# A top-k attention and expert-layer kernel: another latency in its planner, another wait for the first transposes, and SyncE's last reads in another order

## The chip, the cores and the metric

The kernel runs on one core of one Trainium2 chip. The metric is the device time of one launch in microseconds. Before the change its median is 869.37 us over three runs (869.3 to 869.62). The profiled execution spans 867.1 us. The core has five engines that run side by side: TensorE (PE, matmuls and transposes), VectorE (DVE), ScalarE (ACT), GpSimd (POOL) and SyncE (SP, which issues DMAs here).

## The reference

Attention in which each query keeps its 32 best keys, and behind it an expert layer with a squared ReLU:

```python
# q, k, v: (8 batches, 8 heads, 576 positions, 64)
scores = scale * np.matmul(q, k.transpose(0, 1, 3, 2))
kth = np.partition(scores, -top_k, axis=-1)[..., -top_k:-top_k + 1]   # top_k = 32
mask = scores >= kth
scores = np.where(mask, scores, -1000000000.0)
attn = softmax(scores)                      # written out with max, exp and sum
x = np.matmul(attn, v)                      # then (8*576 tokens, 8*64 = 512)
h = x @ w_in                                # 512 -> 2048
g = np.maximum(h, 0.0) ** 2
out = g @ w_out                             # 2048 -> 512
```

## The kernel before

The kernel works in 144 blocks. A block is 128 queries of two heads: PE computes two rows of 576 scores per query into `ps_s`, ACT copies them to `s`, and DVE finds the 32nd largest of each row. It takes the eight largest of a part (`Max`), strikes them out (`MatchReplace`), three times over parts of growing width (104, 124, 272 columns), and then takes the eight largest of all 576 (`kth`). Parts and folds are made with maxima and with integer adds and subtracts on DVE, ACT and GpSimd (`m`, `t1`, `t2`, `f`).

ACT then makes a mask `w` for each of the two heads, PE transposes scores and adds the masks, ACT takes the exponential (`p`), PE multiplies with v (`vb,p`), and the expert layer follows for a chunk of tokens when all four pairs of heads have reached it (`xt,win`, then `wo,g`).

None of this is written in the order in which it runs. Every operation is recorded with an engine, an assumed duration and a priority, and a list scheduler written in Python orders each engine's operations ahead of the launch; semaphores are put in from that order. On the chip each engine runs its list strictly in order. This is the part of the scheduler in which the assumed latency stands:

```python
def schedule(self, t0=0.0, latency=0.12, own=0.07):
    # ... (cut)
                    for v in x.users:
                        left[v] -= 1
                        lat = 0 if x not in v.deps else (own if x.eng != "pe" else .25) if v.eng == x.eng else latency
                        readyat[v] = max(readyat[v], t + lat)
```

Masks and transposes of a block (L720 and L449/L452 in the profile):

```python
                for i in range(2):
                    pl.op("act", .77, tw + .8 * i, lambda i=i: act.activation(
                        at(wt)[:, i, :], at(st)[:, i, :], ACTF.Relu, bias=kth[:, i, n:n + 1], scale=-1.0),
                        r=[st], w=[wt], take=[wt] if i == 0 else [], after=[ks[i]])
    # ... (cut)
            o_t = pl.op("pe", .68, tt, lambda: flip([0, 128, 256, 384], 0), r=[st, wt], w=[e], take=[e, pt])
            o_t = pl.op("pe", .68, tt + .1, lambda: flip([640, 768, 896, 1024], 4), r=[st, wt], w=[e], order=[o_t])
            pl.op("pe", .2, tt + .2, lambda: flip([512], 8), r=[st, wt], w=[e, e9], take=[e9], order=[o_t])
```

The expert layer of a chunk: `xt,win` matmuls, ReLU on ACT, and the square on DVE, GpSimd or ACT. The last chunks have 128 tokens each: 64 matmuls of 128 columns (`xt,win`), four squares, 16 matmuls of 512 columns (`wo,g`), one copy and one store.

```python
                pl.op("act", .19 + w_ / 1200, tf + lag + .5, fr, r=[hh], w=[g])
                if end:                                  # the very last chunk
                    pl.op("dve", ...)                    # g * g
                elif last or i * SQ % 8 < SQ:            # other chunks of the last batch, and some
                    pl.op("gp", ...)                     # g * g
                else:
                    pl.op("act", ...)                    # Square
```

While PE has nothing to do at the start, it plays 87 warm-up matmuls of 512 columns (`ps<-ident_bf`), which write two spare PSUM banks that are also used for transposes of q and k.

At the end a verdict is formed: were 32 keys found in each row in this fast way, and are the sums in range? If not, a fallback program that does it all in a slower way (the `again` plan) is run. Every engine reads the verdict from memory and branches:

```python
        def emit(e, eng):
            em.via(main, e)
            em.emit(main, e, eng)
            if e == "sp":
                for kk, vv in stored(main).items():
                    eng.wait_ge(em.sem(kk), vv)          # all stores of the output
            eng.wait_ge(em.sems["dve"], flagged.idx[1])
            val = eng.value_load(flag[0:1, 0:1], min_val=0, max_val=P)
            with eng.If(val > 0):
                em.emit(again, e, eng)
                # ... (cut)
```

Of the kernel before, what the change touches and what calls it, by code (L numbers as in the profile page):

```python
# [291 lines left out]
def bass_top_k_attn__then__act_relu_squared_kernel(  # L292
# [24 lines left out]
            return nc.alloc_sbuf_tensor(name, shape, dt)  # L317
        return [nc.alloc_sbuf_tensor(f"{name}{i}", shape, dt) for i in range(n)]

    PER = 5.55  # L320
    T0 = 12.0
    LEAD = 39.88
    ME = 21.85
    MQ = 19.61
    MP = 18.0
    MA = 18.27
    SQ = 5.15
    TA = 7.2
    TW = -0.14
    TL = 18.33  # L330
    WARM = 8
    WP = 6.49
    BW = 1
    WSTEP = 1.2
    WEND = 70
    NL = 31.89
    WD = 3.33
    WC = 1.75
    WA = 1.13
    WN = 6  # L340
    NBO = 3.81
    LAG = 12.93
    STEP = 2.98
    LATE = 2.07
    LAGL = 17.86

    ident32 = sb("ident32", [P, P])
    ident_bf = sb("ident_bf", [P, P], BF16)
# [10 lines left out]
    fone = sb("fone", [P, 4])  # L359
# [31 lines left out]
    def tile(nm):  # L391
        return Tile(pools[nm])
# [4 lines left out]
    def bank(t, i=0):  # L397
        return ps32[:, BASE[t.pool.name] + t.slot + i, :]
# [8 lines left out]
    em = Emitter(nc)  # L407
# [48 lines left out]
    def build(full, weights, pl):  # L456
# [129 lines left out]
        def top_k(gi, qks, tg):  # L586
# [53 lines left out]
            ks = []  # L640
# [72 lines left out]
                        eighth(kth, i), at(f)[:, i, :]), hold=[f]))  # L713
            kths.extend(ks)
            tw = tg + PER - TW
            wt = tile("w")
            if not full:

                for i in range(2):
                    pl.op("act", .77, tw + .8 * i, lambda i=i: act.activation(  # L720
                        at(wt)[:, i, :], at(st)[:, i, :], ACTF.Relu, bias=kth[:, i, n:n + 1], scale=-1.0),
                        r=[st], w=[wt], take=[wt] if i == 0 else [], after=[ks[i]])
                return st, wt

            for i in range(2):
                o = pl.op("gp", .75, tw + 1.3 * i, lambda i=i: gp.tensor_scalar(
# [2 lines left out]
                pl.op("gp", .75, tw + 1.3 * i + .65, lambda i=i: gp.tensor_scalar(  # L729
                    at(wt)[:, i, :], at(f)[:, i, :], BIG, at(sh)[:, i:i + 1], ALU.min, ALU.max),  # L730
                    r=[sh], hold=[f], after=[o], w=[wt], take=[wt] if i == 0 else [])
            return st, wt

        minus = neg_bf if full else steep_bf

        def attend(gi, st, wt, tt):

            e, e9, pt = Tile(ps_e), Tile(ps_q), tile("p")

            def flip(cols, i0):  # L740
                sf, wf = (at(t)[:, :, :].rearrange("p i c -> p (i c)") for t in (st, wt))
                outs = [(banks(e)[:, 128 * (i0 + i):128 * (i0 + i) + 128], c, (i0 + i) % 4 == 0)
                        for i, c in enumerate(cols)]
                for o, c, start in outs:
                    tr(o, sf[:, c:c + 128], ident32[:, :], start=start, stop=True)
                for o, c, start in outs:
                    ins = mm(o, wf[:, c:c + 128], minus[:, :], False)
                return ins


            o_t = pl.op("pe", .68, tt, lambda: flip([0, 128, 256, 384], 0), r=[st, wt], w=[e], take=[e, pt])
            o_t = pl.op("pe", .68, tt + .1, lambda: flip([640, 768, 896, 1024], 4), r=[st, wt], w=[e], order=[o_t])
            pl.op("pe", .2, tt + .2, lambda: flip([512], 8), r=[st, wt], w=[e, e9], take=[e9], order=[o_t])
            pl.op("act", 1.15, tt + 1, lambda: act.activation(  # L754
                at(pt)[:, :, :].rearrange("p k q -> p (k q)"), banks(e)[:, 0:2 * S], ACTF.Exp, scale=0.125),
                r=[e, e9], w=[pt])
            return pt
# [57 lines left out]
        def feed(chunk, xt, tm, step):  # L815

            nt = sum(n_ for _, _, n_ in chunk)
            b = chunk[-1][0]
            last, end = b == NB - 1, chunk is CHUNKS[-1]
            kf = max(1, 512 // nt)  # L820
            lag = 0 if end else LAGL if last else LAG
            gs = [tile("g") for _ in range(NFB // kf)]
            for i, g in enumerate(gs):
                hh = Tile(psum)

                def fh(hh=hh, i=i):
                    for f in range(kf):
                        fb = kf * i + f
                        for ct in range(NCT):
                            ins = mm(bank(hh)[:, nt * f:nt * f + nt], win[:, ct, 128 * fb:128 * fb + 128],  # L830
                                     at(xt)[:, ct, 0:nt], ct == 0 and f == 0)
                    return ins

                def fr(hh=hh, g=g):
                    return act.activation(at(g)[:, 0:kf * nt], bank(hh)[:, 0:kf * nt], ACTF.Relu)  # L835

                tf = tm + step * i
                w_ = kf * nt
                ho = pl.op("pe", .03 + kf * 4 * (nt / 2340 + .002), tf + lag, fh, r=[xt], w=[hh], take=[hh, g],
                           after=weights if chunk not in FIRST else weights and weights[NCT * (kf * i // 8):][:NCT],  # L840
                           nbf=tf if not last else 0)
                if chunk in FIRST and weights:
                    first_h.append(ho)
                pl.op("act", .19 + w_ / 1200, tf + lag + .5, fr, r=[hh], w=[g])
                if end:
                    pl.op("dve", .1 + w_ / 1900, tf + lag + .8, lambda g=g: vec.tensor_tensor(
                        at(g)[:, 0:w_], at(g)[:, 0:w_], at(g)[:, 0:w_], ALU.mult), u=[g])
# [45 lines left out]
        for b in range(NB):  # L893
            seq, stages = batch_order(b)
            pairs, held = {}, {}
            last = b == NB - 1
            for hp, gi in seq:
                tg = T0 + PER * state["n"]
                hps = (hp, hp if gi != Z else hp + 1)
                for x in hps:  # L900
                    if x not in pairs:
                        pairs[x] = load_pair(b, x, tg)
                st, wt = top_k(gi, [pairs[x][0] for x in hps], tg)
                if state.get("more"):
                    state.pop("more")()
                tt = tg + PER + 2 - TA - TL * max(0, 1 - (NGRP - state["n"]) / NL)
                pt = attend(gi, st, wt, tt)
                js = [gi] if gi == Z else [g for g in stages if gi in g][0]
                held.setdefault((hp, js[0]), []).append((pt, [pairs[x][1] for x in hps]))
                if gi != js[-1]:  # L910
                    continue
                r0, n_ = 128 * js[0], 128 * len(js) if gi != Z else 64
                i, col = place(b, r0, n_)
                first = xts[i] is None
                if first:
                    xts[i] = tile("xz" if len(CHUNKS[i]) > 1 else "xt")
                collect(gi, held[hp, js[0]], (xts[i], col, first), hp, tt)
                left[i] -= n_ * (2 if gi == Z else 1)
                if left[i] == 0:
# [53 lines left out]
    def verdict(pl, kths, rzs):  # L973
# [11 lines left out]
            fone[:, 1:2], fone[:, 1:2], 1e30, None, ALU.is_gt), after=[e])  # L985
        f = pl.op("dve", .1, 1e6, lambda: vec.tensor_scalar(
            fone[:, 2:3], fone[:, 2:3], 1e-30, None, ALU.is_lt), after=[f])
        g = pl.op("pe", .1, 1e6, lambda: pe.matmul(bank(t)[0:1, 0:3], fone[:, 3:4], fone[:, 0:3],
                                                   start=True, stop=True), w=[t], take=[t], after=[d, e, f])
        return pl.op("dve", .1, 1e6, lambda: vec.tensor_reduce(flag[:, :], bank(t)[0:1, 0:3], AX.X, ALU.max), r=[t])  # L990

# [6 lines left out]
    for o in main.ops[n_pre:]:  # L998
        if o.eng == "sp" and o.takes and o.takes[0].pool.name == "rv":
            o.deps.update(zeros)  # L1000
        if o.eng == "pe":
            o.deps.update(early if n < 7 else early + pre)
            n += 1
    span = main.schedule()
    assert all(o.takes[1].slot < NG - 4 * NWS for o in first_h)
    em.number(main)
    again = Plan()
# [7 lines left out]
    with nc.Block() as blk:  # L1015
        def emit(e, eng):
            em.via(main, e)
            em.emit(main, e, eng)
            if e == "sp":
                for kk, vv in stored(main).items():  # L1020
                    eng.wait_ge(em.sem(kk), vv)
            eng.wait_ge(em.sems["dve"], flagged.idx[1])
            val = eng.value_load(flag[0:1, 0:1], min_val=0, max_val=P)
            with eng.If(val > 0):
                em.emit(again, e, eng)
                if e == "sp":
                    for kk, vv in stored(again).items():
                        eng.wait_ge(em.sem(kk), vv)

        @blk.gpsimd  # L1030
        def _(g_):
            emit("gp", g_)

        @blk.tensor
        def _(pe_):
            emit("pe", pe_)
# [40 lines left out]
```

## Time and profile before

| engine | busy us | share of the 867.1 us | instructions |
|---|---|---|---|
| PE | 823.6 | 95% | 7998 |
| DVE | 824.2 | 95% | 3414 |
| POOL | 788.2 | 91% | 826 |
| ACT | 760.2 | 88% | 1261 |

The DMA engines move 48.21 MB at a mean of 56 GB/s. By the page's chain of work that ended last, DVE holds 66% of the span, PE 21%, ACT 8%, and 5% is "issue".

How to read the lines below: in a timeline a line has start, length, engine, source line, operation, output and inputs with shape, and in brackets the idle time of the engine before it and who ended it. "PE ps L449" is any matmul, "L452" any transpose, for two helper functions issue them all; what they are is told by the tiles behind the arrow. In a row of windows there are the stretch, its length, and busy time with the number of instructions for PE, PEld (the load of weights), DVE, ACT and POOL, then the granted clock, the DMA share and GB/s. A name with a q at the end (SPq, PEldq) is an engine's sequencer.

### The profile page before, as it was taken

What the parts mean: (1) busy time and instruction counts of PE and PEld (TensorE: products, weight loads), DVE (VectorE), ACT (ScalarE), POOL (GpSimd) and SP (SyncE); (2) the same over time, 40 slices, a digit from 0 to 9 for tenths busy, and PEclk for the clock granted to TensorE, in tenths of its full rate; (3) what the DMA queues carried; (4) which work ended last, traced back from release to release, by engine and by line L of the source; (5) the groups of instructions that cost most, each with busy time, mean ns of one, the idle gap of its engine ahead of it and who ended that gap; (6) DMA issues with size and microseconds to landing.
All of it is one profiled execution on the core that took longest, in us unless ns stands there. A gap on an engine that the chain in (4) does not pass through costs nothing.

```text
span 867.1 us, 22631 instructions
## 1 busy us (share of the span) xinstructions
PE 823.6 (95%) x7998; PEld 609.9 (70%) x8057; DVE 824.2 (95%) x3414; ACT 760.2 (88%) x1261; POOL 788.2 (91%) x826
## 2 busy tenths in 40 slices
PE   8898899999999999999999999999999999999996
PEld 3565677667776777767778677776778767687774
DVE  3899999999999999999999999999999999999970
ACT  3788999889998899989999799998989889898873
POOL 6798999999999989999999989999999988998961
PEclk9999999999999999999999999999999999999999
DMA  7583422011310223012130121301231021000001
GB/s 180 120 198 101 126 49 62 27 41 35 91 43 14 60 64 76 21 34 62 33 79 16 39 68 43 97 14 41 57 82 30 14 51 32 26 2 14 26 14 41
DMA packets 126985, 48.21 MB, mean 56 GB/s; under 512 B 119184, under 2 KB 119184, under 8 KB 126864
## 3 DMA queue, kind: packets, MB, share of 16 engines
q1 hardware_dynamic: 126192, 46.52, 21.4%
q8 instruction: 65, 1.06, 0.5%
q14 instruction: 56, 0.46, 0.2%
q10 hardware_dynamic: 672, 0.16, 0.1%
HBM read 37.22 MB, written 9.44 MB: 54 GB/s over the span
## 4 chain that ended last, share of the span: by engine, by line
DVE 66%; PE 21%; ACT 8%; issue 5%; POOL 1%; DVEq 0%; POOLq 0%
DVE f L709 21%; DVE c L705 17%; PE ps L449 15%; DVE kth L712 13%; PE ps L452 5%; DVE ps L678 5%; DVE f L688 5%; DVE m L678 5%; ACT p L754 2%; ACT w L720 1%; ACT s L622 1%; ACT g L835 1%; DVE rzall L783 1%; ACT qk L579 0%; ACT g L852 0%
## 5 line engine op out<-in xcount | busy, mean ns | idle before, releaser
L709 DVE MATCH_REPLACE8 f<-c,f 128x104 f32<-128x104 f32 (+2 forms) x864 | 268.1, 317 | 0.0
L705 DVE MAX8 c<-f 128x8 f32<-128x104 f32 (+2 forms) x864 | 244.7, 321 | 0.1
L720 ACT ACTIVATE w<-s,kth 128x576 bf16<-128x576 f32 x288 | 223.4, 786 | 22.5 <-DVE kth L712 21.6
L452 PE MATMUL ps<-ident,s 128*128 128x128 f32 x1296 | 222.0, 280 | 9.2 <-ACT p L754 5.7
L673 POOL TENSOR_TENSOR t<-s 128x576 int32<-128x576 int32 x144 | 202.5, 1411 | 19.7 <-ACT s L622 19.6
L449 PE MATMUL ps<-qk 64*128 64x64 f32 (+3 forms) x1280 | 207.0, 442 | 2.9 <-DVE m L678 2.5
L712 DVE MAX8 kth<-f 128x8 f32<-128x576 f32 x288 | 208.5, 750 | 0.0
L673 POOL TENSOR_TENSOR f<-t,m 128x576 int32<-128x576 int32 x144 | 203.0, 1410 | 0.0
L449 PEld LDWEIGHTS ps<-qk 64*128 64x128 f32 (+1 forms) x1280 | 128.1, 175 | 77.4 <-issue 60.4
L622 ACT COPY s<-ps 128x1152 f32<-128x1152 f32 x144 | 161.4, 1121 | 22.7 <-PE ps L449 22.4
L754 ACT ACTIVATE p<-ps 128x1152 bf16<-128x1152 f32 x144 | 163.4, 1135 | 13.5 <-PE ps L449 12.6
L452 PEld LDWEIGHTS ps<-ident,s 128*128 128x128 f32 x1296 | 143.1, 141 | 34.2 <-ACT p L754 11.0
L449 PE MATMUL ps<-steep_bf,w 128*128 128x128 bf16 x1296 | 139.9, 219 | 0.0
L673 POOL TENSOR_TENSOR t<-m 128x288 int32<-128x288 int32 x144 | 114.8, 797 | 18.8 <-ACT m L686 14.4
L449 PE MATMUL ps<-wo,g 128*128 128x512 bf16 x517 | 127.6, 379 | 4.1 <-issue 1.0
L449 PE MATMUL ps<-xt,win 128*128 128x256 bf16 (+1 forms) x1152 | 127.0, 261 | 4.1 <-ACT xt L809 2.3
L673 POOL TENSOR_TENSOR f<-t,f 128x288 int32<-128x288 int32 x144 | 114.7, 797 | 0.1
L449 PEld LDWEIGHTS ps<-xt,win 128*128 128x128 bf16 x1152 | 97.4, 98 | 19.6 <-ACT xt L809 3.7
L449 PEld LDWEIGHTS ps<-steep_bf,w 128*128 128x128 bf16 x1296 | 105.1, 100 | 4.0
L849 POOL TENSOR_TENSOR g<-g 128x512 bf16<-128x512 bf16 x92 | 95.3, 1040 | 7.6 <-ACT g L835 7.3
L835 ACT ACTIVATE g<-ps 128x512 bf16<-128x512 f32 x144 | 85.8, 607 | 5.6 <-PE ps L449 4.4
L449 PEld LDWEIGHTS ps<-wo,g 128*128 128x128 bf16 x576 | 51.8, 98 | 48.5 <-ACT g L835 0.5
(67 smaller groups left out, 913.5 us busy)
## 6 DMA issues: line engine op xcount, KB each, us to landing
rv<-in_v_dram SPq DMA_DIRECT2D x64, 128.0 KB, 2.5
out_dram<-o SPq DMA_DIRECT2D x32, 256.0 KB, 2.1
rk<-in_k_dram SPq DMA_DIRECT2D x63, 128.0 KB, 2.5
rq<-in_q_dram SPq DMA_DIRECT2D x62, 128.0 KB, 2.6
g<-in_moe_w_in_dram SPq DMA_DIRECT2D x8, 512.0 KB, 4.3
g<-in_moe_w_out_dram SPq DMA_DIRECT2D x8, 512.0 KB, 3.9
rv<-in_v_dram SPq DMA_DIRECT2D x96, 16.0 KB, 2.2
rq<-in_q_dram SPq DMA_DIRECT2D x32, 32.0 KB, 2.6
```

The costliest lines, as they stand in the source:

```text
L449: return pe.matmul(o, l, r, start=start, stop=stop, skip_group_check=True)
L452: return pe.matmul(o, i, ident, is_transpose=True, skip_group_check=True, **kw)
L622: cp = [pl.op("act", 1.2, tg - LEAD + 1, lambda: act.copy(at(st)[:, :, :], two(banks(ss), SECOND, S)), r=[ss], w=[st])]
L673: return pl.op("gp", dur, prio, lambda: gp.tensor_tensor(o().bitcast(I32), x().bitcast(I32), y().bitcast(I32), op), **kw)
L678: return vec.tensor_tensor(o, two(banks(ss)[:, a:], SECOND + HALF, QUART), two(at(st)[:, 0, HALF + a:], HALF, QUART), ALU.max)
L705: lambda i=i, t=t, c0=c0, c1=c1: vec.max(eighth(t, i), at(f)[:, i, c0:c1]),
L709: lambda i=i, t=t, c0=c0, c1=c1: vec.match_replace(at(f)[:, i, c0:c1], eighth(t, i), at(f)[:, i, c0:c1], NEG), hold=[f])]
L712: ks.append(chain(kth, i, prev[i] + [low], .665, lambda i=i: vec.max(eighth(kth, i), at(f)[:, i, :]), hold=[f]))
L720: pl.op("act", .77, tw + .8 * i, lambda i=i: act.activation(at(wt)[:, i, :], at(st)[:, i, :], ACTF.Relu, bias=kth[:, i, n:n + 1], scale=-1.0),
L754: pl.op("act", 1.15, tt + 1, lambda: act.activation(at(pt)[:, :, :].rearrange("p k q -> p (k q)"), banks(e)[:, 0:2 * S], ACTF.Exp, scale=0 ...
L835: return act.activation(at(g)[:, 0:kf * nt], bank(hh)[:, 0:kf * nt], ACTF.Relu)
L849: pl.op("gp", .15 + w_ / 480, tf + lag + 1, lambda g=g: gp.tensor_tensor(at(g)[:, 0:w_], at(g)[:, 0:w_], at(g)[:, 0:w_], ALU.mult), u=[g])
```

## The change

1. The planner assumes 0.25 us between an operation and one on another engine that needs it, instead of 0.12 us. The order of all five engines is planned anew with it, and the offsets of the priorities (when scores, folds, weights and expert work are wanted) are set anew to go with it.
2. The first four transposes of a block (128-column pieces 0 to 3, all of the first head) wait for the first of the two masks, not for both.
3. SyncE reads the verdict first and waits for the stores afterwards, so that the reading and the branch lie beside the last store. The verdict's matmul no longer has the lowest priority on PE.
4. The squares of the last chunk but one are done by DVE as well.

The diff, with cuts:

```diff
-    PER = 5.55
+    PER = 5.54
-    LEAD = 39.88
-    ME = 21.85
-    MQ = 19.61
+    LEAD = 38.17
+    ME = 19.82
+    MQ = 18.93
-    MA = 18.27
-    SQ = 5.15
+    MA = 21.24
+    SQ = 5.71
-    TW = -0.14
-    TL = 18.33
+    TW = 0.23
+    TL = 15.79
-    WP = 6.49
+    WP = 5.93
-    NL = 31.89
-    WD = 3.33
-    WC = 1.75
+    NL = 36.79
+    WD = 1.68
+    WC = 2.44
-    LATE = 2.07
-    LAGL = 17.86
+    LATE = 2.51
+    LAGL = 21.59
 ...
-            wt = tile("w")
+            wt, masks = tile("w"), []
-                    pl.op("act", .77, tw + .8 * i, lambda i=i: act.activation(
+                    masks[i:] = [pl.op("act", .77, tw + .8 * i, lambda i=i: act.activation(
 ...
-            o_t = pl.op("pe", .68, tt, lambda: flip([0, 128, 256, 384], 0), r=[st, wt], w=[e], take=[e, pt])
+            own = dict(r=[st], hold=[wt], after=ws_[:1]) if ws_ else dict(r=[st, wt])
+            o_t = pl.op("pe", .68, tt, lambda: flip([0, 128, 256, 384], 0), w=[e], take=[e, pt], **own)
 ...
+            direct = chunk in CHUNKS[-2:]
-                if end:
+                if direct:
                     pl.op("dve", .1 + w_ / 1900, ...
 ...
-        g = pl.op("pe", .1, 1e6, lambda: pe.matmul(bank(t)[0:1, 0:3], fone[:, 3:4], fone[:, 0:3],
+        g = pl.op("pe", .1, 0, lambda: pe.matmul(bank(t)[0:1, 0:3], fone[:, 3:4], fone[:, 0:3],
 ...
-    span = main.schedule()
+    span = main.schedule(latency=.25)
 ...
-            if e == "sp":
-                for kk, vv in stored(main).items():
-                    eng.wait_ge(em.sem(kk), vv)
             eng.wait_ge(em.sems["dve"], flagged.idx[1])
             val = eng.value_load(flag[0:1, 0:1], min_val=0, max_val=P)
             with eng.If(val > 0):
+                if e == "sp":
+                    for kk, vv in stored(main).items():
+                        eng.wait_ge(em.sem(kk), vv)
                 em.emit(again, e, eng)
                 # ... (cut)
+            if e == "sp":
+                for kk, vv in stored(main).items():
+                    eng.wait_ge(em.sem(kk), vv)
```

More of the change, by code (lines that the diff above doesn't have):

```diff
@@ L715, in top_k @@
             tw = tg + PER - TW
-            wt = tile("w")
+            wt, masks = tile("w"), []
             if not full:
                 for i in range(2):
-                    pl.op("act", .77, tw + .8 * i, lambda i=i: act.activation(
+                    masks[i:] = [pl.op("act", .77, tw + .8 * i, lambda i=i: act.activation(
                         at(wt)[:, i, :], at(st)[:, i, :], ACTF.Relu, bias=kth[:, i, n:n + 1], scale=-1.0),
-                        r=[st], w=[wt], take=[wt] if i == 0 else [], after=[ks[i]])
-                return st, wt
+                        r=[st], w=[wt], take=[wt] if i == 0 else [], after=[ks[i]])]
+                return st, wt, masks
             for i in range(2):
@@ L731, in top_k, with attend @@
                     r=[sh], hold=[f], after=[o], w=[wt], take=[wt] if i == 0 else [])
-            return st, wt
+            return st, wt, masks
         minus = neg_bf if full else steep_bf
-        def attend(gi, st, wt, tt):
+        def attend(gi, st, wt, tt, ws_):
             e, e9, pt = Tile(ps_e), Tile(ps_q), tile("p")
@@ L902, in build @@
                         pairs[x] = load_pair(b, x, tg)
-                st, wt = top_k(gi, [pairs[x][0] for x in hps], tg)
+                st, wt, ws_ = top_k(gi, [pairs[x][0] for x in hps], tg)
                 if state.get("more"):
@@ L906, in build @@
                 tt = tg + PER + 2 - TA - TL * max(0, 1 - (NGRP - state["n"]) / NL)
-                pt = attend(gi, st, wt, tt)
+                pt = attend(gi, st, wt, tt, ws_)
                 js = [gi] if gi == Z else [g for g in stages if gi in g][0]
```

## The prediction

> **What bounds the kernel now.** I read the page's busy times and slices first, then a table of windows, then the idle times of VectorE (DVE) in order of time, then the last instructions of TensorE (PE), ScalarE (ACT) and SyncE. From the page:
>
> ```profile
> span 867.1 us, 22631 instructions
> PE 823.6 (95%) x7998; PEld 609.9 (70%) x8057; DVE 824.2 (95%) x3414; ACT 760.2 (88%) x1261; POOL 788.2 (91%) x826
> DVE  3899999999999999999999999999999999999970
> ```
>
> DVE is full except in the first two slices and in the last two. The windows say how full (busy us, instructions; in the order PE, PEld, DVE, ACT, POOL):
>
> ```profile
> 0.00:10.00 10.00, 7.24 (x29) 3.09 (x29) 0.69 (x1) 2.49 (x5) 4.28 (x30) 1.00 0.59 137
> 10.00:20.00 10.00, 9.52 (x43) 3.96 (x42) 6.30 (x25) 4.29 (x7) 8.63 (x9) 1.00 0.88 208
> 20.00:30.00 10.00, 9.11 (x56) 5.06 (x54) 7.46 (x29) 8.01 (x13) 5.79 (x7) 1.00 0.47 107
> ...
> 500.00:600.00 100.00, 96.34 (x958) 73.50 (x966) 99.85 (x412) 92.53 (x155) 93.83 (x96) 1.00 0.22 54
> ...
> 850.00:867.00 17.00, 10.36 (x94) 6.24 (x92) 2.00 (x5) 4.01 (x7) 1.66 (x2) 0.95 0.10 36
> ```
>
> From about 30 to 836 us DVE sets the pace: 144 blocks with no idle worth the name. Its whole idle time is 867.1 - 824.2 = 42.9 us: 9.3 + 3.7 + 2.5 in the first 30 us, about 2.5 scattered, and some 25 after the last threshold. So the change can win at the start, at the end, and hardly between. The start, from DVE's timeline (start, length, what, idle before it and who ended it):
>
> ```profile
> 10.44 0.47 DVE L678 TENSOR_TENSOR ps<-ps,s 128x288 f32<-128x288 f32 x1 [2.93 <-ACT s L622]
> 15.42 0.47 DVE L678 TENSOR_TENSOR ps<-ps,s 128x288 f32<-128x288 f32 x1 [3.12 <-ACT s L622]
> ...
> 26.07 0.47 DVE L678 TENSOR_TENSOR ps<-ps,s 128x288 f32<-128x288 f32 x1 [1.40 <-ACT p L754]
> ...
> 29.49 0.47 DVE L678 TENSOR_TENSOR ps<-ps,s 128x288 f32<-128x288 f32 x1 [1.11 <-ACT s L622]
> ```
>
> Blocks 1 to 4 each wait for their scores, which wait for PE, which plays warm-up matmuls in between. The end, from the timeline of all engines; K, the end of the last threshold, is 834.85 + 1.42 = 836.27:
>
> ```profile
> 834.85 1.42 DVE L712 MAX8 kth<-f 128x8 f32<-128x576 f32 x2
> ...
> 847.85 5.53 PE L449 MATMUL ps<-xt,win 128*128 128x128 bf16 x96 [0.63 <-ACT g L835]
> ...
> 853.43 6.86 PE L449 MATMUL ps<-wo,g 128*128 128x512 bf16 x31
> ...
> 860.33 0.59 ACT L869 COPY o<-ps 128x512 f32<-128x512 f32 x1 [2.00 <-PE ps L449]
> ```
>
> After K it is PE that bounds: 24 us of expert-layer matmuls with under 1.5 us of gaps. Then SyncE, from its lines in the source view (ns min/median/max, when):
>
> ```profile
> L1022 SPq EVENT_SEMAPHORE  x1: 1962/1962/1962, 861.3 to 861.3; - x1
> L1023 SPq TENSOR_LOAD <-flag x1: 465/465/465, 863.3 to 863.3; - x1
> L1024 SPq COMPARE_BRANCH  x1: 45/45/45, 864.2 to 864.2; - x1
> L1024 PEldq COMPARE_BRANCH  x1: 4025/4025/4025, 861.5 to 861.5; - x1
> L1015 PEldq DRAIN  x1: 73/73/73, 865.6 to 865.6; - x1
> L1015 SPq DRAIN  x1: 53/53/53, 866.9 to 866.9; - x1
> ```
>
> The last store is issued at 860.94; SyncE waits 1.96 us for it, only then loads the verdict, branches at 864.2, and drains at 866.9. Everybody else has been done since 865.6.
>
> [...]2.7 us from SyncE's branch to its drain, with transfers in the instruction queues, although the branch itself takes 0.045 us. [...]
>
> **The change part by part.**
>
> *SyncE reads the verdict first.* Removed from the end: load, register operations, branch and fetch standing behind the store's 1.96 us. Now SyncE loads at 861.27 (issue 860.94 + 0.33), branches 0.9 us later (863.3 to 864.2 before) at 862.15 and is ready 2.7 us later, at 864.85; the store landed at 863.3. But PE drained at 865.6, 5.0 us after it read the flag at 860.6. The verdict's matmul now stands among the tail's matmuls instead of behind them, so PE reads the flag when its last matmul is issued, some 0.5 us earlier: about 865.1. PE, not SyncE, then ends the kernel, at about 865.1 + 0.2. Worth 867.1 - 865.3 = -1.8 us.
>
> *The start, walked through the changed instruction order with durations of this trace.* The transposes of the rest of the first queries now stand before the first scores: one more warm-up, then 0.69 us to the scores, which start at about 8.7 (7.89 before). Copy to s: 10.1 to 11.2; DVE starts block 1 at 11.25 (10.44): +0.8. Between first and second scores there are now 11 warm-ups instead of 8, but they alternate between two PSUM banks (each waits for the last but one); such a run went at 0.22 us each in the trace (13 from 14.14 on), while the 8, which mostly wait for the one just before, took 3.09 us. Second scores: 10.0 + 11 x 0.22 + 0.2 = 12.65 (12.87). DVE gets block 2 at 15.2 (15.42). It then stalls about 0.3 us, because ACT now converts a weight tile (1.05 us) before the copy into m that DVE needs; block 1 is done at 20.85 (20.80). Block 3's scores need the second pair's keys: I get 20.85 for their start (21.87), s ready at 23.4, a stall of 0.7 in place of 1.40. Block 4's s is ready when DVE gets there, about 28.7: about 0.1 in place of 1.11. Block 3 then ends at 33.8 against 34.88 before. The start is worth -1.1 us; the two later stalls (0.92 at 42.0 and 0.86 at 65.5) may go or stay, -0.3.
>
> *Twice the latency, new offsets.* No instruction is added: the same 87 warm-ups, the same matmuls, the same 144 blocks on DVE. Only their order and waits differ. For the last 30 blocks I added up, at each block's transposes, how much expert work (0.061 us per 128-column matmul, 0.215 per 512-column one, from 6.87 us for 32) is still to come. In the changed order PE is level with before around blocks 100 to 120, 1 to 6 us ahead from 124 to 136, and 2.6 us ahead at the last block. From its first transposes on, PE has: before, 48 x 0.215 + 7.5 for 128 + 3.1 of attention = 20.9 (trace: 839.49 to 860.30); now, 36 x 0.215 + 7.5 + 2.9 = 18.2. But 12 of the 512-column matmuls have moved to just before, and there the stretch grows from 4.3 (835.20 to 839.49) to 5.5. Net -1.4 us, if PE reaches the last block but one as early as now. Its idle share there is only 2 to 3%, so I credit -1.2.
>
> *Masks, squares.* The first four transposes of a block wait for the first of its two masks (0.786 us each): PE may start 0.8 us earlier, which DVE doesn't see; credit within the 1.2. Squares of the last chunk but one go from GpSimd (4 x 1.04) to DVE (4 x 0.46 = 1.9 us), all behind K, where DVE idles for over 20 us: 0.
>
> *Middle.* DVE has no idle to win. The order can only add stalls; I allow +0.3.
>
> Sum: -1.8 - 1.1 - 0.3 - 1.2 + 0.3 = -4.1, so 869.37 - 4.1 = 865.3.
>
> **Rivals.** (1) The planned latency is now too long. The trace has 0.03 to 0.06 us between the end of a producer and the start of its consumer (s ends 10.41, DVE starts 10.44), so 0.12 was ample already. Then operations are put later than needed, buffers are held longer, and DVE stalls a few tenths here and there: +2 to +4 us over 144 blocks, and the total stays at 867 to 869. For it: 533 waits of DVE on other engines in the changed order against 470. Against: real durations vary, and a looser plan is sturdier. (2) PE is the true bound all along (97% busy in the middle), and its 2 to 3% of idle, some 20 us from 100 to 800, comes from tight plans. Then the looser order lowers PE's idle by a quarter or so, the backlog at K shrinks, and the end gains 4 to 5 instead of 1.2: 861 to 862. For it: PE carries 24 us of work past K. Against: DVE at 100% paces PE's inputs. (3) SyncE's move gives less, since PE's branch (4.0 us) is fetched as late as before, or the fetches collide with the store: -1.0 instead of -1.8.
>
> **Range and chances.** Rival 1 in full gives 868.5, rival 2 in full 861; both ends look equally likely, so 861.0 to 868.8 at 8 in 10. Faster by 2% would need 852, more than all that start and tail can give: 0.02. Slower by 2% would need 17 us of new stalls: 0.02.
>
> **What would show it.** Right: SyncE's load of the flag right after the last store's issue and PE's drain the last but one event, with about 4.4 us from the last copy's end to the end of the span (6.2 before); DVE's first block at 11.25, later than before, but threshold 3 done at about 33.8; DVE's idle between 40 and 830 at 2 to 3 us; 23.4 us or so from K to the last copy's end (24.65 before). Wrong: many short DVE idles in the middle (rival 1), K to last copy under 20 us (rival 2), or K itself later than 836 (my walk of the start).

## The result, and the profile after

The changed kernel takes 873.81 us (median of 4 runs, 872.61 to 874.18); the kernel before took 869.38 beside it (869.3 to 869.62). The ratio is 1.0048, with a 95% interval of 1.0031 to 1.0066: a loss of some 4 us, where 865.3 had been predicted, and outside the 861.0 to 868.8 given for it.

First the page of the changed kernel:

```profile
span 872.3 us, 22749 instructions
PE 828.6 (95%) x8057; PEld 612.2 (70%) x8057; DVE 825.8 (95%) x3418; ACT 759.1 (87%) x1258; POOL 787.6 (90%) x825
DVE  3999999999999999999999999999999999899892
```

DVE is now below 9 tenths in two slices of the middle (the 8s near the end: 742 to 763 and 807 to 829 us). The table of windows of the changed kernel puts sizes to it (columns as before: length, then busy us and instructions of PE, PEld, DVE, ACT, POOL):

```profile
0.00:10.00 10.00, 7.25 (x26) 2.88 (x27) 0.69 (x1) 2.02 (x5) 5.13 (x31) 1.00 0.60 136
10.00:20.00 10.00, 9.82 (x50) 4.53 (x47) 5.59 (x24) 4.90 (x8) 7.55 (x7) 1.00 0.94 224
20.00:30.00 10.00, 8.98 (x56) 5.02 (x55) 9.17 (x36) 8.07 (x13) 6.92 (x8) 1.00 0.52 132
30.00:100.00 70.00, 62.00 (x535) 42.56 (x534) 66.76 (x275) 59.97 (x96) 65.65 (x67) 1.00 0.59 154
100.00:480.00 380.00, 363.47 (x3608) 275.21 (x3610) 379.54 (x1579) 346.38 (x573) 360.37 (x364) 1.00 0.19 47
480.00:620.00 140.00, 136.11 (x1290) 100.55 (x1291) 138.00 (x579) 126.02 (x208) 129.50 (x130) 1.00 0.20 49
620.00:700.00 80.00, 77.05 (x790) 59.26 (x789) 80.00 (x334) 73.45 (x121) 77.47 (x79) 1.00 0.15 38
700.00:845.60 145.60, 143.38 (x1499) 108.37 (x1497) 138.72 (x578) 127.24 (x222) 132.81 (x141) 1.00 0.10 26
```

And the same view of the kernel before, for three of these stretches and for all from 100 us to K (the end of the last threshold, at 836.27):

```profile
30.00:100.00 70.00, 61.85 (x552) 42.76 (x552) 68.05 (x281) 59.44 (x95) 64.32 (x65) 1.00 0.57 145
...
480.00:620.00 140.00, 135.53 (x1316) 101.97 (x1323) 139.85 (x582) 127.41 (x213) 131.64 (x133) 1.00 0.21 51
...
700.00:836.27 136.27, 133.11 (x1395) 101.40 (x1405) 136.10 (x572) 122.71 (x216) 123.47 (x132) 1.00 0.09 26
...
100.00:836.27 736.27, 713.24 (x7068) 538.66 (x7124) 735.93 (x3066) 673.96 (x1122) 697.20 (x709) 1.00 0.18 44
```

Length minus the DVE column is DVE's idle time. From 700 us to K it was 136.27 - 136.10 = 0.17 before and is 145.60 - 138.72 = 6.88 now; from 480 to 620 it was 0.15 and is 2.00. DVE's busy time up to K is the same in both kernels (818.43 and 818.46 us), so all of the delay of K is idle time. The start and the end of the changed kernel, from DVE's timeline and from the timeline of all engines:

```profile
12.07 0.47 DVE L678 TENSOR_TENSOR ps<-ps,s 128x288 f32<-128x288 f32 x1 [3.60 <-ACT s L622]
15.91 0.47 DVE L678 TENSOR_TENSOR ps<-ps,s 128x288 f32<-128x288 f32 x1 [1.99 <-ACT s L622]
...
24.04 0.47 DVE L678 TENSOR_TENSOR ps<-ps,s 128x288 f32<-128x288 f32 x1 [0.75 <-ACT s L622]
```

```profile
843.31 0.66 PE L452 MATMUL ps<-ident,s 128*128 128x128 f32 x4 [0.35 <-ACT p L755]
...
844.18 1.42 DVE L712 MAX8 kth<-f 128x8 f32<-128x576 f32 x2
...
845.26 2.75 PE L449 MATMUL ps<-wo,g 128*128 128x512 bf16 x12
...
848.17 0.63 PE L452 MATMUL ps<-ident,s 128*128 128x128 f32 x4
...
862.88 3.62 PE L449 MATMUL ps<-wo,g 128*128 128x512 bf16 x16
...
866.53 0.59 ACT L871 COPY o<-ps 128x512 f32<-128x512 f32 x1 [2.86 <-PE ps L449]
```

K is at 844.18 + 1.42 = 845.60, the last copy's end at 867.12. Last, the sequencers' lines of the changed kernel in the source view (ns min/median/max, when):

```profile
L1022 PEldq TENSOR_LOAD <-flag x1: 488/488/488, 864.2 to 864.2; - x1
L1022 SPq TENSOR_LOAD <-flag x1: 512/512/512, 867.5 to 867.5; - x1
L1023 PEldq COMPARE_BRANCH  x1: 3588/3588/3588, 865.1 to 865.1; - x1
L1023 SPq COMPARE_BRANCH  x1: 50/50/50, 868.4 to 868.4; - x1
L1033 SPq EVENT_SEMAPHORE  x1: 17/17/17, 871.8 to 871.8; - x1
```

SyncE loads the flag right behind its last store and branches at 868.4; the next instruction in its list, the wait for the stores that now stands behind the branch (L1033), comes at 871.8 and takes 17 ns. PE's branch is over at 865.1 + 3.6 = 868.7.

The two profiles, stage by stage (spans 867.1 and 872.3, idle times from the windows):

| stage | before, us | after, us | difference | predicted |
|---|---|---|---|---|
| DVE idle, 0 to 30 us | 15.55 | 14.55 | -1.0 | -1.1 |
| DVE idle, 30 to 100 us | 1.95 | 3.24 | +1.3 | -0.3 |
| DVE idle, 100 us to K | 0.34 | 9.35 | +9.0 | +0.3 |
| K to the last copy's end | 24.65 | 21.52 | -3.1 | -1.2 |
| last copy's end to the end of the span | 6.18 | 5.18 | -1.0 | -1.8 |
| sum | | | +5.2 | -4.1 |

**Where the new idle time comes from.** DVE's timeline of the changed kernel shows the long ones:

```profile
578.11 0.47 DVE L678 TENSOR_TENSOR ps<-ps,s 128x288 f32<-128x288 f32 x1 [2.00 <-ACT p L755]
...
738.38 0.09 DVE L709 MATCH_VALUE_LOAD f<-c,f 128x8 f32 x1 [1.56 <-POOL f L673]
...
746.32 0.09 DVE L709 MATCH_VALUE_LOAD f<-c,f 128x8 f32 x1 [2.02 <-POOL f L673]
...
811.87 0.09 DVE L709 MATCH_VALUE_LOAD f<-c,f 128x8 f32 x1 [1.39 <-POOL f L673]
```

The first can be followed in the timeline of all engines just before it:

```profile
575.41 0.66 PE L452 MATMUL ps<-ident,s 128*128 128x128 f32 x4
...
575.87 1.18 ACT L622 COPY s<-ps 128x1152 f32<-128x1152 f32 x1
...
576.24 0.22 PE L449 MATMUL ps<-steep_bf,w 128*128 128x128 bf16 x1
...
576.86 1.21 ACT L755 ACTIVATE p<-ps 128x1152 bf16<-128x1152 f32 x1
...
578.11 0.47 DVE L678 TENSOR_TENSOR ps<-ps,s 128x288 f32<-128x288 f32 x1 [2.00 <-ACT p L755]
```

A block's ninth transposed piece and a later block's first fold (L678 into `ps`) share one PSUM bank, and the exponential p has to read it out before the fold may write. PE is done with the ninth piece at 576.46, but ACT copies the next scores first, and p ends at 578.07. DVE, which had run out of other work at 576.1, waits 2.0 us. That exchange on ACT is worth 0.4 of them (p could have begun at 576.46 and not at 576.86); the rest is the lateness of the ninth piece itself, which isn't followed further here. GpSimd's stalls are the larger part, 5.5 of the 9.35 us. The longest of them:

```profile
743.37 0.80 POOL L673 TENSOR_TENSOR t<-m 128x288 int32<-128x288 int32 x1
...
744.12 1.41 POOL L673 TENSOR_TENSOR f<-t,m 128x576 int32<-128x576 int32 x1
...
745.49 0.80 POOL L673 TENSOR_TENSOR f<-t,f 128x288 int32<-128x288 int32 x1
```

The last of these folds is the one that DVE waits for until 746.32. It seems to have had its inputs at 744.17, but another fold of 1.41 us stands ahead of it in GpSimd's list. In both cases each engine does work that is in its list, in the order of the list; it is the order that is worse. The other stalls were not followed.

### The profile page after: what moved, and what is told of

It is laid out like the page before. It is cut to its first block, busy times and chain, and to the rows that moved or that the text cites. A ratio compares the mean times of both kernels' runs of the same rounds, so it can differ in the third digit from the quotient of the medians.

```text
span 872.3 us, 22749 instructions
## 1 busy us (share of the span) xinstructions
PE 828.6 (95%) x8057; PEld 612.2 (70%) x8057; DVE 825.8 (95%) x3418; ACT 759.1 (87%) x1258; POOL 787.6 (90%) x825
## 4 chain that ended last, share of the span: by engine, by line
DVE 61%; PE 21%; ACT 7%; issue 6%; POOL 4%; DVEq 0%; POOLq 0%
DVE f L709 20%; PE ps L449 17%; DVE c L705 16%; DVE kth L712 11%; PE ps L452 5%; DVE ps L678 5%; DVE f L688 4%; DVE m L678 4%; ACT p L755 2%; POOL t L673 2%; POOL f L673 1%; ACT s L622 1%; ACT w L720 1%; ACT g L837 1%; DVE rzall L784 1%
## 5 line engine op out<-in xcount | busy, mean ns | idle before, releaser
L720 ACT ACTIVATE w<-s,kth 128x576 bf16<-128x576 f32 x288 | 221.7, 785 | 24.5 <-DVE kth L712 23.6
L673 POOL TENSOR_TENSOR t<-s 128x576 int32<-128x576 int32 x144 | 203.2, 1413 | 15.8 <-ACT s L622 15.6
L449 PE MATMUL ps<-wo,g 128*128 128x512 bf16 x576 | 138.8, 379 | 0.1
```

The lines of the kernel that those rows point to most:

```text
L449: return pe.matmul(o, l, r, start=start, stop=stop, skip_group_check=True)
L673: return pl.op("gp", dur, prio, lambda: gp.tensor_tensor(o().bitcast(I32), x().bitcast(I32), y().bitcast(I32), op), **kw)
L720: masks[i:] = [pl.op("act", .77, tw + .8 * i, lambda i=i: act.activation(at(wt)[:, i, :], at(st)[:, i, :], ACTF.Relu, bias=kth[:, i, n:n + ...
```

## The experiments

**1. The parts, one by one.** SyncE's order alone (`sp_first`), the planned latency alone (`lat_only`), the changed kernel with the old offsets, and the changed kernel with the old latency.

```diff
# sp_first: the kernel before with the change's end and the verdict's matmul
-        g = pl.op("pe", .1, 1e6, lambda: pe.matmul(...
+        g = pl.op("pe", .1, 0, lambda: pe.matmul(...
-            if e == "sp":            # all stores awaited here, ahead of the flag
+            if e == "sp":            # ... now behind the branch
# lat_only: the kernel before
-    span = main.schedule()
+    span = main.schedule(latency=.25)
# after_oldparams: the changed kernel with the 14 offsets of the kernel before
# after_lat12: the changed kernel
-    span = main.schedule(latency=.25)
+    span = main.schedule(latency=.12)
```

> The kernel before with part 3 of the change alone: SyncE reads the verdict first, the verdict's matmul loses its lowest priority. The plan's latency and offsets stay. In the changed kernel 5.2 us lie between the last copy's end (867.12) and the end of the span (872.3), 6.2 before, so every theory expects about -1.0 us: 868.4. If it is worth my first figure, 867.6.

> The kernel before with the planner's latency 0.25 in place of 0.12, nothing else. Theory A (the new offsets put expert work ahead of transposes, PE is late, VectorE starves from 700 us on): no loss, 866 to 870. Theory B (the longer latency itself makes a worse order): 872 to 876, with VectorE idle 5 us or more between 100 us and the last threshold. Theory C (every new plan is a draw, whatever was changed): anything from 866 to 876, and none of the four runs of this call lines up with its ingredients.

> The changed kernel with all 14 offsets put back to their old values; latency 0.25, own-mask wait, squares and SyncE's order as changed. Theory A: the loss is gone, 866 to 869, VectorE's idle between 100 us and the last threshold under 2 us. Theory B: still slow, 872 to 876.

> The changed kernel with the planner's latency put back to 0.12, all else as changed. Theory A: still slow, 872 or more, since the offsets stay. Theory B: the loss is gone, 866 to 869.

| kernel | us | ratio to before, 95% interval | DVE idle, 100 us to K |
|---|---|---|---|
| sp_first | 867.75 | 0.9978 [0.9971, 0.9985] | - |
| lat_only | 885.34 | 1.0179 [1.0152, 1.0206] | 15.64 |
| after_oldparams | 880.02 | 1.0125 [1.0108, 1.0142] | 13.28 |
| after_lat12 | 869.27 | 1.0001 [0.9993, 1.001] | 1.03 |

The row from 100 us to K in the windows of `lat_only`, then that of `after_lat12`:

```profile
100.00:851.22 751.22, 716.88 (x7031) 539.84 (x7087) 735.58 (x3056) 671.78 (x1115) 695.15 (x705) 1.00 0.17 43
```

```profile
100.00:836.54 736.54, 714.34 (x7063) 538.37 (x7115) 735.51 (x3066) 671.08 (x1117) 697.73 (x709) 1.00 0.17 43
```

So the new offsets don't do the harm: with the old ones the changed kernel is 6 us worse. The latency does. With everything else of the change in place, going from 0.25 back to 0.12 takes 8.3 of the 9.35 us of idle time away, and 4.5 us of the kernel's time: the end from K to the last copy, 21.5 us in the changed kernel, is 26.6 in `after_lat12`. Theory A falls. Theory B has the direction, but both kernels that it covers with the old offsets lie above its 872 to 876. SyncE's order is the one part that gains alone, and by nearly the first figure (867.75 against 867.6), not the -1.0 us. What the latency changes is seen in ACT's waits from 100 us to K (total us, times, longest), in the kernel before, the changed one, and with the latency alone, in this order:

```profile
ACT s L622 <- PE ps L449: 12.2, 25, 1.3
```

```profile
ACT s L622 <- PE ps L449: 25.7, 38, 2.0
```

```profile
ACT s L622 <- PE ps L449: 36.0, 54, 2.4
```

ACT comes to copy scores that PE hasn't computed yet, two to three times as long. Scores are the first link of a block; what comes behind them on ACT, in order, comes late as well, and GpSimd's folds and DVE after it. That this wait is what stalls DVE is argued, not shown: `lat_to_gp` below loses 4.5 us with 12.6 us of such waits, little more than the 12.2 of the kernel before.

**2. Which dependence.** The longer latency for one receiving engine only (here PE; likewise DVE, ACT, GpSimd), on the kernel before:

```diff
-  lat = ... if v.eng == x.eng else latency
+  lat = ... if v.eng == x.eng else (.25 if v.eng == "pe" else latency)
```

> The kernel before; the planner assumes 0.25 us only where the consumer is on TensorE, 0.12 elsewhere. With 0.25 everywhere it took 885.3. Theory P (the plan believes that transposes come free later, so TensorE is given expert matmuls to fill the gap, and is busy with them when the transposes are free on the chip): most of the loss, 878 to 885. Theory L (no single edge: the loop from threshold over mask, transposes and exponential back to VectorE's first fold has five edges that each add 0.13 us, and only their sum matters): 869 to 874, and the same for each engine. Theory C (every new plan is a draw): no pattern over the four.

> 0.25 us only into VectorE. Theory V (the plan lets VectorE itself idle, and puts everything else later): most of the loss, 878 to 885. Theory P: none, 869 to 871. Theory L: 869 to 874.

> 0.25 us only into ScalarE (score copies, masks, exponentials). Theory P and theory V: none, 869 to 871. Theory L: 869 to 874, and the most of the four, since three of the loop's edges end on ScalarE.

> 0.25 us only into GpSimd (the integer folds and squares), which lies beside the loop. All of P, V and L: none, 868 to 871. Over 873 speaks for C.

| receiver with 0.25 | us | ratio | DVE idle, 100 us to K |
|---|---|---|---|
| PE | 873.64 | 1.0046 [1.0023, 1.0068] | 3.81 |
| DVE | 874.41 | 1.0067 [1.0044, 1.009] | 6.41 |
| ACT | 879.73 | 1.0122 [1.0093, 1.0151] | 8.55 |
| GpSimd | 873.64 | 1.0057 [1.0033, 1.0081] | 3.30 |

No single dependence carries it. Every one loses 4 us or more, even GpSimd's, and ACT's, where most links of a block end, loses most. Theories P and V fall, and theory L with them (873.6 for GpSimd, 879.7 for ACT); GpSimd's 873.6 is the sign that was named for theory C. That each loses about as much as the whole change, or more, raised a second theory: the old offsets fit one plan, and any other plan, whatever its latency, is a fresh draw that they weren't fitted to.

**3. How much, and in which direction.** The kernel before with latencies of 0.06, 0.13 and 0.40 us, and with the old latency but one offset moved by 0.1 us.

```diff
# lat06, lat13, lat40: the kernel before
-    span = main.schedule()
+    span = main.schedule(latency=.06)        # or .13, .4
# lead_jit: the kernel before
-    LEAD = 39.88
+    LEAD = 39.98
```

> The kernel before with a planned latency of 0.13 us instead of 0.12, nothing else. Dose theory (the loss is the size of the latency, worth about 16 us for +0.13): +0.01 costs about 1.2 us at most, 869 to 871. Draw theory (the fourteen offsets were fitted to one plan, and any other plan is a fresh draw): 872 to 876, as high as a quarter-size change of the latency on one engine gave.

> The kernel before with a planned latency of 0.06 us instead of 0.12. Dose theory: tighter than before, so no later than 869, perhaps 865. Draw theory: 872 to 880, although the latency is smaller.

> The kernel before with a planned latency of 0.40 us. Dose theory: 16 us for +0.13 becomes some 30 us for +0.28, about 895 to 905. Draw theory: 875 to 890, no worse than the 885.3 of 0.25.

> The kernel before with one offset moved by 0.1 us (LEAD 39.88 to 39.98), latency 0.12 as before. Dose theory: 869 to 870, nothing of the latency has changed. Draw theory: 872 to 876, if that shift changes the order of the middle at all.

| kernel | us | ratio | DVE idle, 100 us to K | ACT waits for scores, 100 us to K |
|---|---|---|---|---|
| lat06 | 884.41 | 1.0175 [1.0122, 1.0228] | 5.08 | 13.2 |
| before (0.12) | 869.09 | 1 | 0.34 | 12.2 |
| lat13 | 872.97 | 1.004 [1.002, 1.006] | 4.13 | 22.5 |
| lat40 | 879.54 | 1.0119 [1.0089, 1.0148] | 12.07 | 37.1 |
| lead_jit | 869.05 | 1.0 [0.999, 1.001] | 0.25 | 10.7 |

0.01 us of latency costs nearly as much as the whole change, a smaller latency costs 15 us, and 0.40 costs less than 0.25. A theory in which time grows with the latency alone falls with these. The second theory's ranges hold at 0.13 and 0.40; at 0.06 the time lies above its 872 to 880. `lead_jit` is a miss as a test: the new value left PE's instruction order the same over the first half and changed it only in places later, so it was hardly another plan. The idle column keeps something of the first theory, though: it is 5.1 us or less at 0.13 and below, and 12 and 15.6 at 0.40 and 0.25.

**4. The same waits with and without a new plan.** The own-mask wait was put into `sp_first` in two ways. In `own_emit` the planner still believes that a block's first transposes wait for both masks, and the second wait is taken out only afterwards: all engines keep the order of `sp_first`. In `own_only` the planner knows of it (and SyncE is left as before), at latency 0.12 and with the old offsets. `sp_direct` puts the squares of the last chunk but one on DVE; `after_lat24` is the changed kernel with 0.24.

```diff
# own_emit
     span = main.schedule()
+    for o, m in trims:               # o: a block's first transposes, m: its second mask
+        o.deps.discard(m)
     em.number(main)                  # waits are set from here on
# sp_direct
-                if end:
+                if chunk in CHUNKS[-2:]:
                     pl.op("dve", ...)                    # g * g
# after_lat24: the changed kernel
-    span = main.schedule(latency=.25)
+    span = main.schedule(latency=.24)
```

> sp_first (867.8) with the first half of a block's transposes waiting for their own mask alone, but with the plan made as if they waited for both: every engine's order stays that of sp_first, and only that wait is shorter. If the order is what counts, the shorter wait is worth nothing where VectorE never idles: 867 to 868.5. If the own mask is a gain of itself, 864 to 866.

> The kernel before with the same waits for the own mask, but told to the planner, which then plans anew at latency 0.12 with the old offsets. Draw theory: a new plan that the offsets were not fitted to, 872 to 878. Rival (the mask's part is harmless, only latencies do harm): 868 to 869.5.

> sp_first with the second-last chunk's squares moved from GpSimd to VectorE; the plan differs only in its last stretch. If that move is what shortens the end from the last threshold on (21.5 against 24.7 us in the changed kernel), 865 to 866.5; if that end is shorter only because the thresholds come late there, 867 to 869.

> The changed kernel with a planned latency of 0.24 us instead of 0.25. Draw theory: its fourteen new offsets were fitted to the plan of 0.25, so 0.24 is a fresh draw and later than 873.8: 875 to 882. Dose theory (a latency of 0.25 is in itself too loose, 0.12 gives 869.3): 873 to 874.

| kernel | us | ratio | K | DVE idle, 100 us to K |
|---|---|---|---|---|
| own_emit | 867.52 | 0.9979 [0.9971, 0.9987] | 836.59 | 0.34 |
| own_only | 875.43 | 1.0073 [1.0053, 1.0093] | 840.81 | 3.67 |
| sp_direct | 867.77 | 0.9981 [0.9973, 0.9989] | 836.79 | 0.34 |
| after_lat24 | 877.08 | 1.0092 [1.0072, 1.0112] | 845.05 | 8.53 |

The row from 100 us to K in the windows of `own_emit`, then that of `own_only`:

```profile
100.00:836.59 736.59, 717.57 (x7127) 538.76 (x7124) 736.25 (x3067) 674.47 (x1123) 698.13 (x710) 1.00 0.18 44
```

```profile
100.00:840.81 740.81, 716.95 (x7093) 537.25 (x7092) 737.14 (x3068) 672.89 (x1119) 694.96 (x706) 1.00 0.18 44
```

PE, DVE, ACT and GpSimd do the same work in both to within 3.2 us (DVE to 0.9), but the second stretch is 4.2 us longer. The own-mask wait is worth nothing by itself (867.52 against 867.75 for `sp_first`), and the plan that it brings loses 6 us. The squares on DVE are worth nothing either. And the changed kernel's own latency is as sharp a choice as the old one: 0.24 in place of 0.25 costs 3 us more.

**5. Offsets fitted to the new program.** `refit` has SyncE's order, the own mask known to the planner, and the squares on DVE, at 0.12 us, with offsets set anew by a search for the plan with the earliest end. `refit3` has the same parts, the own mask as in `own_emit`, and another set of offsets.

```diff
# refit, against own_only with SyncE's order and the squares on DVE
-    LEAD = 39.88
-    ME = 21.85
-    MQ = 19.61
-    MA = 18.27
+    LEAD = 42.1
+    ME = 18.27
+    MQ = 16.11
+    MA = 20.11
 ...                                          # 16 more offsets
# refit3: LEAD 40.43, ME 21.59, MQ 40.1, MA 18.18, 15 more
```

> SyncE's order, the own mask (told to the planner) and the squares on VectorE, at a latency of 0.12 us, with offsets set anew for exactly this program: the planner's own end of the last threshold is 831.2 us, against 836.9 with the old offsets and 832.2 for the kernel before. Draw theory: fitted offsets bring the loss of own_only (875.4) back in full, and the end gains 1.5 us from SyncE: 865 to 867.5. Rival (the own mask, planned, does harm that offsets can't mend): 869 to 873.

> The same parts, but the own mask is not told to the planner (plan as if both masks were waited for), with another set of offsets fitted to that, latency 0.12: the planner's own last threshold at 831.5 us. Draw theory: 865 to 867.5, level with refit; if the plan's own number says nothing of the chip, anything from 867 to 875.

`refit` takes 867.58 us (ratio 0.9992, 0.9975 to 1.0008), `refit3` 870.67 (1.0014, 1.0001 to 1.0027). The windows of `refit`:

```profile
30.00:100.00 70.00, 59.17 (x532) 42.17 (x533) 66.51 (x278) 57.62 (x94) 62.42 (x64) 0.98 0.52 128
100.00:838.51 738.51, 719.50 (x7150) 540.14 (x7148) 737.26 (x3069) 677.34 (x1124) 700.71 (x713) 1.00 0.18 45
838.51:865.70 27.19, 21.59 (x244) 15.43 (x241) 6.64 (x21) 11.69 (x23) 1.78 (x4) 1.00 0.09 33
```

From 875.4 to 867.6 is 7.8 us, of which SyncE's order accounts for some 1.6 (869.38 - 867.75); about 6 come from the offsets. So the parts of the change are harmless once the plan fits. `refit` lies a hair above its 865 to 867.5, and its median hides two groups: with a granted clock of 0.999 five executions took 866.4 to 866.8 us, with 0.995 or 0.996 five took 869.5 to 869.8 and a sixth 875.5. But the search gained little more: the planner's own figure for K was 1.0 us better than for the kernel before (831.2 against 832.2), and on the chip K was 2.2 us worse (838.51 against 836.27), though the end from K on was 3.6 us shorter (27.19 against 30.83; 29.11 in `own_emit`, which has SyncE's order too). A part of the 2.2 can be the clock's, 0.98 from 30 to 100 us in the first row, where DVE idles 3.49 us (1.95 in the kernel before). `refit3` missed the same range with a clock of 1.00 there: K planned at 831.5, measured at 838.29. Of all versions `sp_first`, `own_emit` and `sp_direct` beat both kernels clearly, by 0.2% and by the same amount: the old plan with SyncE's new order.

## Why the prediction was wrong

**The step that failed** is the one called "Middle": "DVE has no idle to win. The order can only add stalls; I allow +0.3." From 100 us to K the stalls are +9.0. I had seen that no instruction is added, that DVE's work stays the same (818.46 against 818.43, right), and that it has no idle to win (right), and then sized the loss as if an order that is as good were sure. The runs show two things in place of the +0.3. The latency: every plan with 0.24 us or more on all dependences leaves DVE idle for 8.5 to 15.6 us between 100 us and K (five plans), every new plan with 0.13 or less for 1.0 to 5.1 (six plans; `own_emit`, `sp_direct` and, for most of the way, `lead_jit` keep the old order). With the change's own offsets 0.25 instead of 0.12 costs 8.3 us of idle time and 4.5 us in all. And the fit: at the same latency, or 0.01 from it, a new plan with the old offsets loses 4 to 6 us (`lat13`, `own_only`). Beside the new plan it is 3 (`after_lat24`), and all of that behind K: K is at 845.05, and the last copy ends 24.76 us later. But not every new plan loses so much: `after_lat12` is one too, with offsets that came with 0.25, and DVE idles 1.03 us in it. Nor do the new offsets serve 0.25 alone. They are worth 6.2 us there (880.02 against 873.81; 9.35 us of idle against 13.28) and, by an estimate, some 4.5 at 0.12 (`own_only` less the 1.6 us of SyncE's order, 873.8, against 869.27). They get back much of what the change costs, not all.

**Rival 1** (the planned latency is too long) was right in direction and in its sign in the profile, stalls in many places in the middle, and too small: it gave +2 to +4 and 867 to 869. Its reason, operations put later than needed, is seen in ACT's waits for scores, 25.7 against 12.2 us. That a latency of 0.06, which by that reason should be harmless or better, loses 15 us shows that it isn't the whole reason.

**Rival 2** (PE the true bound, and a looser order lowers its idle time) falls. PE's idle time from 100 us to K rose from 23.0 to 25.6 us, and by more than that: 59 matmul records are missing from the trace of the kernel before, and `own_emit`, with the same order and none missing, has 19.0.

**The start** came out: -1.0 for the first 30 us against -1.1, in part by luck. Block 1 began at 12.07 (11.25 predicted), because PE was slow for longer in this execution (see the last section): five transposes of k, which block 1 needs, took 1.33 us and not 0.86, and ended at 7.96 us and not at 6.98. But block 2's stall was 1.99 (3.12 before), block 3's 0.75 (0.7 predicted), block 4's, 1.11 before, was gone, and block 3 ended at 33.94 (33.8 predicted). (The second scores of my walk add up to 12.62, not 12.65, and the net of the tail to -1.5, not -1.4; nothing hangs on it.) The gain goes with the latency: in the five plans with 0.24 or more DVE idles 13.9 to 14.6 us of the first 30, in `after_lat12` 15.97. The -0.3 for the two later stalls was wrong: +1.3, part of the same failure as the middle.

**SyncE** gave -1.0 of the predicted -1.8 between the last copy and the end. This is rival 3 in size, not in its first reason. I let PE end the kernel, at 5.0 us after it reads the flag. PE's branch ended at 868.7, and SyncE ended it, with 3.4 us from its branch to its next instruction (868.4 to 871.8) against the 2.7 of the kernel before. In those stretches the instruction queues (q8 and q14) moved 3 packets, and 5 in the kernel before; that SyncE waits there for instructions to be fetched was my inference, and no run shows it. That such a fetch collided with the store, rival 3's second reason, isn't excluded (73 packets of the store's queue, q1, lie in the 3.4 us, none in the 2.7); but `refit` branches as early, 1.3 us behind its last copy, and takes 2.7. `own_emit` gets the full amount: its last copy ends at 861.24 in a span of 865.7, 4.5 us (4.4 expected for this step), and `sp_first` alone is 1.6 us faster than the kernel before.

**The tail** was better than predicted, -3.1 against -1.2. The stretch from the last block's first transposes to PE's end is 866.50 - 848.17 = 18.3 us, against 18.2 predicted and 20.8 before. What I had charged against it, 12 matmuls moved in front of those transposes, did come (845.26), but lengthened the stretch from the transposes of the block before to 848.17 - 843.31 = 4.9 us and not to 5.5 (4.3 before). And the transposes of the block before began 2.3 us ahead of K, 1.1 in the kernel before: the +1.2 us that I had left out by letting PE reach the last block but one as early as now. It isn't the stalls of DVE in themselves that give PE this lead: with 8.53 us of them `after_lat24` needs 24.76 us from K to the last copy, and `refit` with 1.25 needs 22.66. The squares play no part (`sp_direct`: 29.7 us from K to the end, 29.1 in `own_emit`, and 24.65 to the last copy in both).

**What stays open.** A 0.06 latency loses 15 us though ACT's waits for scores stay at 13.2. In its profile (880.6 against 867.1 us) 3.6 us are more idle time of DVE between 30 and 100 us, 4.7 from there to K, 3.1 more busy time of DVE up to K with the same instructions, and 1.9 from K to the last copy; I haven't found which part of its order does that. The granted clock is an untested rival for parts of such losses: from 30 to 100 us it was 0.95 in `lat06` and 0.98 in `lat_to_pe`, `lat_to_act` and `lat_to_gp`; `lat_only` has 0.98 from 100 to 200 us and from 400 to 500. Up to K it was 1.00 in every stretch read of the two kernels, `after_oldparams`, `after_lat12`, `after_lat24`, `lat13` and `own_only`, so what is read from these doesn't hang on it. With single plans at each value the latency's share and the fit's can't be parted to better than a few us, and no search for offsets was run at 0.25.

## What to carry to other kernels

Where four engines are 87 to 95% busy, as in these two kernels, and each works through its list in order, an instruction order is a tuned object: equal work and equal counts say nothing of its stalls, and a planner's constant (0.01 us of latency here, +4 us) is as large an edit as a rewrite. So keep the order fixed when you want to know what one wait is worth: plan with the old dependences, then take the wait out. And a planner's own end is a coarse guide: the change's program with the old offsets it put 4.7 us later than the kernel before (836.9 against 832.2), and `own_only` was 4.5 later at K; but an order that it thought 0.7 us better (`refit3`) was 2 us worse up to the last threshold.

## What the runs showed of the hardware

In these profiles PE is slow at first, for a time that differs between executions, while the granted clock shows nothing of it (1.00 from 0 to 30 us in all four named here). The same single transpose at 5.0 us took 0.27 us in the kernel before and 0.42 in the changed one, in `own_emit` and in `sp_first`; the five transposes behind it took 0.86, 1.33, 0.86 and 1.41. In the profiled execution of `sp_first`, whose own stages are therefore not compared above, the first scores took 2.50 us, and in that of `own_emit`, with the same order, 1.34. First `sp_first`, then `own_emit`, from PE's timeline:

```profile
9.06 2.50 PE L449 MATMUL ps<-qk 64*128 64x64 f32 x8
...
17.35 2.50 PE L449 MATMUL ps<-qk 64*128 64x64 f32 x8
```

```profile
8.38 1.34 PE L449 MATMUL ps<-qk 64*128 64x64 f32 x8
...
13.36 1.35 PE L449 MATMUL ps<-qk 64*128 64x64 f32 x8
```

The page's row for the clock shows a 9 in every slice of `sp_first`. Four transposes took 1.20 us there at 11.49 and 0.65 at 23.60, so the slow time ended between 19.8, the end of the second scores, and 23.6 us; K came at 842.82, and at 836.59 in `own_emit`. A granted clock below 1.00 stands in other runs, 0.98 in `refit` and 0.95 in `lat06` from 30 to 100 us; what it did to single matmuls isn't shown.

The time from a branch over the fallback program to an engine's next instruction isn't the same in all profiles: 2.7 us on SyncE in the kernel before and in `refit` (862.5 to 865.2), 3.4 in the changed kernel; and PE's branch instruction took 3.4 (`sp_first`) to 4.1 us (`sp_direct`). With one profile for each kernel, whether it differs by kernel or by execution isn't shown.
